# First keys on ScalarE's queue, zero products between the first scores, evenly spread weights, and the last pair but one normalized through DRAM

## The chip, the cores and the metric

The kernel runs on one core of one Trainium2 chip. The metric is the device time of one execution in microseconds (us), as the median of several. Engines are named as in the profile: PE is TensorE's matmul, PEld its weight load, DVE is VectorE, ACT is ScalarE, POOL is GpSimd, SP is SyncE. Each engine works through its own instructions strictly in the order in which the program lists them, so one that waits holds back all that stand behind it.

## What is computed

Three layers follow each other. Attention runs over 2 batches of 12 heads, 448 positions and head size 64, with a soft cap; a gated MLP with a gelu, a layer norm and a product over positions comes next; the third is a gated layer with a convolution over three positions.

```python
scores = scale * np.matmul(q, k.transpose(0, 1, 3, 2))
scores = cap * np.tanh(scores / cap)
attn = np.exp(scores - scores.max(-1, keepdims=True))
attn = attn / (attn.sum(-1, keepdims=True) + 1e-09)
x = np.matmul(attn, v)                      # heads side by side: (2, 448, 768)
h = gelu_tanh(x @ w_in); u, v = h[..., :512], h[..., 512:]
x = x + (u * (einsum('ts,bsd->btd', w_sg, layer_norm(v) * g_ln) + b_sg)) @ w_out
h = np.maximum(x @ w2_in, 0)
c = conv3(h, conv_w)                        # over positions, per channel
out = (h * sigmoid(c)) @ w2_out
```

## The kernel before

**Precision.** Every operand of the large products is split into a rounded high part and a low remainder; `mm3` and `scores` make one product of three matmuls (high by high, high by low, low by high). The weights come as 64-bit floats; `decode` turns a piece of them into such a pair in steps on ACT and DVE (`f` tiles; a piece of `w_in` is 128 rows by 512 columns).

**Attention** works on twelve pairs of heads, N = 0 to 11; pairs 0 to 5 are batch 0. `load(n)` issues five transfers on SP's queue: the queries of the two heads and three pieces of the key tile `kr`. `prep_q` and `prep_k` split them into `Q` and `K`. For pair 0 the queries are not scaled, and the high part of the keys is cast by ACT instead of DVE. A pair is done in two halves, which are the steps R = 2N and 2N+1 of the main loop. `scores(N, half)` makes the scores of two groups of keys in PSUM (`sc`, one buffer); ACT takes their tanh and then exp into `raw`. For pair 0, and for it alone, tanh and exp are done group by group (groups g = 0 to 3), and the matmuls of a group wait until the tanh of the group ahead has read the `sc` tile. `values(N, half)` multiplies `raw` with the values into `pv`, and gathers the sums of the exponentials into `su` by products with ones; for the first half DVE first adds the two groups up in `sm`. It runs one step behind `scores`, and from R = 13 on two steps behind. In the gaps PE makes the first three units of the next layer (`FILL`, tile `mo`). Ten matmuls on a tile of zeros (`wz`, written to `wps`) keep PE at work ahead of the first scores.

**Normalization.** `norm` copies `su` to `se` (DVE) and `pv` to `E` (ACT). After every second pair the sums of both go through DRAM: POOL's queue gathers them (`ss`), DVE adds the guard and takes reciprocals, POOL's queue writes them to DRAM (`d`) and broadcasts them back to 64 partitions each (`rb`, four transfers), and DVE multiplies `E` with `rb`; the product is split into `X`, the input of the next layer. These steps come 3, 4 and 11 ticks of the loop later (two ticks for each R). The last two pairs, N = 10 and 11 (`NFAST = 2`), take `norm_pe`: DVE adds the guard and takes reciprocals of the whole 128 x 224 tile, four matmuls with `sel` spread them over the partitions (`rp`, in the bank of `su`), DVE multiplies.

**Order.** The code issues work in the order of the loop; a scheduler then sets each engine's order, and `ordered` and `pin` chain some instructions to the one before. `WIN` says at which step (half steps of pairs, in pairs) each of the twelve pieces of `w_in` is requested; the decoding follows 3, 4 and 5 ticks later. `conv_w` (24 columns) and `g_ln` are requested at R = 1 by `columns`.

After attention, the units `u_unit`, `v_unit`, `sg_unit`, `o_unit`, then `h_unit` and `f_unit` are long rows of matmuls with small work on DVE and ACT beside them. The fourth `u_unit` stands right behind attention, the first `v_unit` (L585) behind the second `rp`.

Of the kernel before, what the change touches and what calls it, by code (L numbers as in the profile page):

```python
# [16 lines left out]
P = 128  # L17
# [14 lines left out]
NFAST = 2  # L32
# [7 lines left out]
WIN = (0, 1.5, 3, 4, 5, 6, 6, 8, 8.5, 9.5, 10, 10)  # L40
# [6 lines left out]
def stages(  # L47
# [169 lines left out]
    def attention(att, psa):  # L217
# [12 lines left out]
        def load(n):  # L230
            b, p = divmod(n, NPAIR)
            qr = att.tile([P, S], F32, tag="qr", name="qr", bufs=2)
            kr = kraw[n % 2]
            for h in range(2):
                r = slice(h * D, (h + 1) * D)
                nc.sync.dma_start(qr[r], qT[b, p, r, h])
            nc.sync.dma_start(kr[:D, :S], kT[b, p, :D, 0])
            nc.sync.dma_start(kr[D:, :ST], kT[b, p, D:, 1, D:])
            nc.sync.dma_start(kr[D:, S:], kT[b, p, D:, 1, :D])
            qraw[n] = qr, kr  # L240
# [23 lines left out]
        def prep_k(n):  # L264
            _, kr = qraw.pop(n)
            K = Kt[n % 2]
            lastv[0] = split(kr, K[:, 0], K[:, 1], "a" if n == 0 else "v")
# [26 lines left out]
        raws, acc, held, pairs = {}, {}, {}, []  # L294
        lastm = [None]

        def ordered(*args, **kw):

            with pin(lastm):
                lastm[0] = T.matmul(*args, **kw)  # L300


        def scores(N, half):
# [11 lines left out]
            for g in range(2 * half, 2 * half + 2):  # L315
# [11 lines left out]
                if N == 0:  # L327
                    soft(slice(t, t + (2 if g < 3 else 1)))
            if N:
                soft(slice(0, 4 - half))  # L330
# [37 lines left out]
        def norm(N, ps, su):  # L368
# [13 lines left out]
            if j == 0:  # L382
                return
            ss = att.tile([P, 14], F32, tag="ss", name="ss", bufs=2)
            G.dma_start(ss, se[::32])
            rb = att.tile([P, 2, S], F32, tag="rb", name="rb", bufs=2)

# [3 lines left out]
            def s1():  # L391
# [3 lines left out]
                ds.append(dr.tile([2, 2, 2, S // 2], F32, tag="d", name="d"))  # L395
                d = ds[0]
                G.dma_start(d.rearrange("h f j (p c) -> (h f j p) c", c=14), ss)

            def s1b():
                (d,) = ds  # L400
                for h in range(2):
                    for i in range(2):
# [5 lines left out]
            def s2():  # L408
                with pin(lastv):
                    V.tensor_tensor(out=e, in0=e, in1=rb, op=ALU.mult)  # L410
                with pin(lasta):
                    lastv[0] = split(e, X[:, 0, p - 1 : p + 1, b], X[:, 1, p - 1 : p + 1, b], "a")
# [26 lines left out]
        for R in range(2 * NN + LAGS[1]):  # L439
# [6 lines left out]
            if R < 2 * NN:  # L446
                if half == 0 and N + 2 < NN:
                    load(N + 2)
                scores(N, half)
# [430 lines left out]
```

## Time and profile before

| | |
|---|---|
| median of 3 runs | 350.95 us (349.65 to 352.41) |
| the profiled execution | 349.8 us, of which the span of the profile is 347.9 us |
| PE busy | 328.6 us, 94% of the span |
| DVE busy | 252.9 us, 73% |
| ACT busy | 225.5 us, 65% |
| POOL busy | 32.7 us, 9% |

The profile shows one execution. Times in it count from the start of the span; the 1.9 us between span and time lie outside it. A row of the timeline gives the start, the duration, the engine, the line and operation, and in brackets how long the engine had been idle before it and what ended the wait. Matmuls of one row can overlap. The granted clock of PE (PEclk) is 1.00 at 2.4 GHz and 0.50 at 1.2 GHz.

### The profile page before, as it was taken

The numbers are of one execution on the slowest core, as the hardware profiler recorded it, in microseconds if no ns is written. First come the engines' busy times: TensorE is split into PE (matmuls) and PEld (weight loads), VectorE is DVE, ScalarE is ACT, GpSimd is POOL, SyncE is SP. The second block draws the span as 40 slices with busy tenths as digits, with TensorE's granted clock in tenths as the row PEclk, the third lists the DMA queues.
The fourth block names the chain that finished last, engine by engine and source line by source line (L and its number), as shares of the span: only waits on it lengthen the run. The fifth ranks groups of instructions, "written<-read, shape, count | busy, mean of one in ns | idle before, by whom it ended". The sixth has DMA issues, their size and how long they took to land. (4 is left out here: it accounts for less than half of the span.)

```text
span 347.9 us, 5121 instructions
## 1 busy us (share of the span) xinstructions
PE 328.6 (94%) x1812; PEld 250.5 (72%) x1812; DVE 252.9 (73%) x491; ACT 225.5 (65%) x362; POOL 32.7 (9%) x67
## 2 busy tenths in 40 slices
PE   6699999997999899999999999999999999999992
PEld 4344444543446376898889999999999999999992
DVE  3365888977699545999899679997995999980000
ACT  2868899996899333766776565465775988873110
POOL 3000310403130303021110100000000000000000
PEclk9599999999999999999999999999999999999999
DMA  3895484646422213321323466000275113012211
GB/s 109 254 237 174 128 217 145 186 93 192 113 75 61 74 35 104 94 71 53 99 75 96 132 177 245 2 0 8 85 239 216 32 60 90 3 54 106 81 53 35
DMA packets 18538, 37.43 MB, mean 108 GB/s; under 512 B 3888, under 2 KB 9032, under 8 KB 18504
## 3 DMA queue, kind: packets, MB, share of 16 engines
q1 hardware_dynamic: 17192, 34.64, 32.8%
q0 software_dynamic: 1312, 2.38, 2.7%
q8 instruction: 16, 0.26, 0.3%
q14 instruction: 18, 0.15, 0.1%
HBM read 34.18 MB, written 2.79 MB: 106 GB/s over the span
## 5 line engine op out<-in xcount | busy, mean ns | idle before, releaser
L300 PE MATMUL sc<-Q,K 64*128 64x448 f32 (+1 forms) x252 | 40.5, 403 | 5.9 <-ACT raw L312 4.0
L96 PE MATMUL mo<-X,WI 128*128 128x448 f32 x126 | 46.1, 367 | 0.0
L97 PE MATMUL mo<-X,WI 128*128 128x448 f32 x126 | 45.9, 366 | 0.0
L98 PE MATMUL mo<-X,WI 128*128 128x448 f32 x126 | 45.9, 365 | 0.0
L300 PE MATMUL pv<-raw,V 128*64 128x448 f32 (+1 forms) x168 | 45.1, 579 | 0.0
L300 PEld LDWEIGHTS sc<-Q,K 64*128 64x128 f32 (+1 forms) x252 | 25.2, 193 | 20.9 <-ACT raw L312 8.1
L313 ACT ACTIVATE raw<-raw,one 128x1792 f32<-128x1792 f32 (+3 forms) x26 | 39.1, 1502 | 0.6
L138 DVE SCALAR_TENSOR_TENSOR f<-f 128x512 uint32<-128x512 uint32 (+3 forms) x57 | 30.7, 548 | 10.8 <-ACT f L131 8.2
L312 ACT ACTIVATE raw<-sc 128x1792 f32<-128x1792 f32 (+1 forms) x22 | 32.4, 1475 | 8.7 <-PE sc L300 8.7
L128 ACT ACTIVATE f<-f 128x512 f32<-128x512 f32 (+3 forms) x57 | 30.6, 542 | 10.8 <-DMA f<-in_w_out_dram 5.5
L97 PE MATMUL mo<-HG,W 128*128 128x448 f32 x96 | 34.8, 365 | 0.0
L98 PE MATMUL mo<-HG,W 128*128 128x448 f32 x96 | 34.7, 365 | 0.0
L96 PE MATMUL mo<-HG,W 128*128 128x448 f32 x96 | 34.1, 365 | 0.0
L141 DVE SCALAR_TENSOR_TENSOR f<-f 128x512 uint32<-128x512 uint32 (+3 forms) x57 | 30.7, 548 | 0.2
L300 PEld LDWEIGHTS pv<-raw,V 128*64 128x64 f32 (+1 forms) x168 | 12.0, 147 | 22.2 <-issue 18.6
L96 PEld LDWEIGHTS mo<-X,WI 128*128 128x128 f32 x126 | 23.6, 187 | 2.4 <-DVE u L177 0.4
L97 PEld LDWEIGHTS mo<-X,WI 128*128 128x128 f32 x126 | 23.7, 188 | 2.0
L98 PEld LDWEIGHTS mo<-X,WI 128*128 128x128 f32 x126 | 23.6, 188 | 2.0
L765 ACT ACTIVATE o<-mo 128x448 f32<-128x448 f32 x12 | 6.3, 540 | 26.3 <-PE mo L98 18.6
L131 ACT ACTIVATE f<-f 128x256 uint32<-128x256 uint32 (+2 forms) x44 | 22.5, 511 | 0.0
L97 PEld LDWEIGHTS mo<-HG,W 128*128 128x128 f32 x96 | 18.0, 188 | 1.4
L96 PEld LDWEIGHTS mo<-HG,W 128*128 128x128 f32 x96 | 18.0, 188 | 1.4
(140 smaller groups left out, 645.1 us busy)
## 6 DMA issues: line engine op xcount, KB each, us to landing
f<-in_w_in_dram SPq DMA_DIRECT2D x24, 512.0 KB, 4.8
f<-in_w_out_dram SPq DMA_DIRECT2D x24, 256.0 KB, 4.6
V<-in_vL_dram SPq DMA_DIRECT2D x12, 256.0 KB, 3.9
f<-in_w_out_dram SPq DMA_DIRECT2D x8, 384.0 KB, 3.1
qr<-in_qT_dram SPq DMA_DIRECT2D x24, 112.0 KB, 3.5
out_dram<-o SPq DMA_DIRECT2D x12, 224.0 KB, 1.9
rb<-d POOLq DMA_DIRECT2D x20, 112.0 KB, 3.8
kr<-in_kT_dram SPq DMA_DIRECT2D x12, 112.0 KB, 3.1
```

The lines of the kernel that those rows point to most:

```text
L96: matmul(ps, lhsT=whi, rhs=xhi, start=start, stop=False)
L97: matmul(ps, lhsT=whi, rhs=xlo, start=False, stop=False)
L98: matmul(ps, lhsT=wlo, rhs=xhi, start=False, stop=stop)
L128: A.activation(f(h), f(h), AF.Copy, scale=2.0**-112)
L131: A.activation(l, l, AF.Copy, scale=0.93 * 2.0**-29)
L138: V.scalar_tensor_tensor(out=l, in0=h, scalar=3, in1=l, op0=ALU.logical_shift_left, op1=ALU.bitwise_or)
L141: V.scalar_tensor_tensor(out=l, in0=h, scalar=0x80000000, in1=l, op0=ALU.bitwise_and, op1=ALU.bitwise_or)
L300: lastm[0] = T.matmul(*args, **kw)
L312: A.activation(raw[:, t], ps[:, t, :S], AF.Tanh, **sc)
L313: lasta[0] = A.activation(raw[:, t], raw[:, t], AF.Exp, scale=capc)
L765: A.activation(o, ps, AF.Copy, scale=0.5)
```

## The change

The three key transfers of pair 0 are issued by ACT's queue instead of SP's, and the high part of these keys is cast by DVE like all others. After each of the first two groups of scores PE gets five matmuls on the tile of zeros (`idle`). The first half of the values of pair 0 moves from behind its last group of scores to between groups 2 and 3. `WIN` asks for a piece of `w_in` every 0.9 pairs. `NFAST` becomes 1: pair 10 is normalized through DRAM, by itself, with half-size `ss`, `d` and two `rb` transfers.

```diff
-NFAST = 2
+NFAST = 1
+IDLE = 5
-WIN = (0, 1.5, 3, 4, 5, 6, 6, 8, 8.5, 9.5, 10, 10)
+WIN = tuple(0.9 * j for j in range(12))
...
-            nc.sync.dma_start(kr[:D, :S], kT[b, p, :D, 0])
-            nc.sync.dma_start(kr[D:, :ST], kT[b, p, D:, 1, D:])
-            nc.sync.dma_start(kr[D:, S:], kT[b, p, D:, 1, :D])
+            dma = (nc.sync if n else nc.scalar).dma_start
+            dma(kr[:D, :S], kT[b, p, :D, 0])
+            dma(kr[D:, :ST], kT[b, p, D:, 1, D:])
+            dma(kr[D:, S:], kT[b, p, D:, 1, :D])
...
-            lastv[0] = split(kr, K[:, 0], K[:, 1], "a" if n == 0 else "v")
+            lastv[0] = split(kr, K[:, 0], K[:, 1])
...
+        idle = psm.tile([P, 512], F32, tag="mo", name="idle")[:, :S]
...
-        def scores(N, half):
+        def scores(N, half, between=None):
...
                 if N == 0:
                     soft(slice(t, t + (2 if g < 3 else 1)))
+                    for _ in range(IDLE if g < 2 else 0):
+                        ordered(idle, lhsT=wz[:, :P], rhs=wz, start=True, stop=True)
+                if between and g == 2:
+                    between()
...
-            if j == 0:
+            last = N == B * NPAIR - NFAST - 1
+            if j == 0 and not last:
                 return
-            ss = att.tile([P, 14], F32, tag="ss", name="ss", bufs=2)
-            G.dma_start(ss, se[::32])
+            m = j + 1
+            ss = att.tile([P, 14], F32, tag="ss", name="ss", bufs=2)[:, : 7 * m]
+            G.dma_start(ss, se[::32, :m])
             rb = att.tile([P, 2, S], F32, tag="rb", name="rb", bufs=2)
+            eb, rb = e[:, :m], rb[:, :m]
...
-                    for i in range(2):
+                    for i in range(m):
...
-                scores(N, half)
+                if R == 1:
+                    scores(N, half, lambda: values(0, 0))
+                    done += 1
+                else:
+                    scores(N, half)
```

The order on PE at the start, from the products of zeros to the second pair's first scores (`K_87` holds the keys of pair 0, `K_88` those of pair 1; `x` counts instructions in a row), before:

```order
L279 MATMUL wps<-wz 128x448 x10
L300 MATMUL sc<-Q,K_87 128x448 x21
L300 MATMUL pv<-raw,V 64x448 x4
L300 MATMUL su<-sm,ones_138 32x224 x4
L300 MATMUL sc<-Q,K_88 128x448 x12
```

and now:

```order
L283 MATMUL wps<-wz 128x448 x10
L305 MATMUL sc<-Q,K_87 128x448 x6
L305 MATMUL idle<-wz 128x448 x5
L305 MATMUL sc<-Q,K_87 128x448 x6
L305 MATMUL idle<-wz 128x448 x5
L305 MATMUL sc<-Q,K_87 128x448 x6
L305 MATMUL pv<-raw,V 64x448 x4
L305 MATMUL su<-sm,ones_138 32x224 x4
L305 MATMUL sc<-Q,K_87 128x448 x3
L305 MATMUL sc<-Q,K_88 128x448 x12
```

The one row of 21 score matmuls is cut into four groups, with zero products behind the first two and the first values and sums ahead of the last.

The order on DVE at the start, from the constants (`one`) to the first `sm`; `f_155` (`f_156` in the changed kernel) is the first piece of `w_in` and the 24 columns of `f_189` (`f_200`) are `conv_w`, before:

```order
L205 TENSOR_TENSOR one<-one 128x1
L207 TENSOR_SCALAR one<-one 128x1
L93 TENSOR_TENSOR K_87<-kr_89,K_87 128x512
L258 TENSOR_SCALAR Q<-qr,one 128x448
L259 SCALAR_TENSOR_TENSOR Q<-qr,one,Q 128x448
L90 CAST K_88<-kr_90 128x512
L93 TENSOR_TENSOR K_88<-kr_90,K_88 128x512
L133 TENSOR_SCALAR f_155<-f_155 128x512
L133 TENSOR_SCALAR f_189<-f_189 128x24
L333 TENSOR_TENSOR sm<-raw 128x896
```

and now:

```order
L260 TENSOR_TENSOR Q<-qr,Q 128x448
L209 TENSOR_SCALAR one<-one 128x1
L92 CAST K_87<-kr_89 128x512
L95 TENSOR_TENSOR K_87<-kr_89,K_87 128x512
L262 TENSOR_SCALAR Q<-qr,one 128x448
L263 SCALAR_TENSOR_TENSOR Q<-qr,one,Q 128x448
L92 CAST K_88<-kr_90 128x512
L95 TENSOR_TENSOR K_88<-kr_90,K_88 128x512
L135 TENSOR_SCALAR f_156<-f_156 128x512
L135 TENSOR_SCALAR f_200<-f_200 128x24
L342 TENSOR_TENSOR sm<-raw 128x896
```

The cast of the first keys has come to DVE, behind the constants and the queries; `sm` stands behind the same work on `conv_w` as before.

The order on DVE in the middle, at the multiplication of pairs 2 and 3 (`E<-E,rb`) and what stands between it and the next `sm`, before:

```order
L410 TENSOR_TENSOR E<-E,rb 128x896
L138 SCALAR_TENSOR_TENSOR f_626<-f_626 128x512
L141 SCALAR_TENSOR_TENSOR f_624<-f_624 128x512
L141 SCALAR_TENSOR_TENSOR f_626<-f_626 128x512
L147 CAST WI_76<-f_624 128x512
L147 CAST WI_77<-f_626 128x512
L150 TENSOR_TENSOR WI_76<-f_624,WI_76 128x512
L333 TENSOR_TENSOR sm<-raw 128x896
```

and now:

```order
L423 TENSOR_TENSOR E<-E,rb 128x896
L149 CAST WI_77<-f_618 128x512
L152 TENSOR_TENSOR WI_77<-f_618,WI_77 128x512
L342 TENSOR_TENSOR sm<-raw 128x896
L92 CAST K_88<-kr_90 128x512
```

Of two pieces of `w_in` that were decoded there together, one is left; the other has moved behind the next `sm`.

The order on PE at the end of attention, around the normalization of pair 10, before:

```order
L300 MATMUL su<-raw,ones_136 32x224 x2
L300 MATMUL su<-raw,ones_137 32x224 x2
L300 MATMUL pv<-raw,V 64x448 x4
L429 MATMUL rp<-r,sel 64x224 x4
L300 MATMUL su<-sm,ones_138 32x224 x4
L300 MATMUL mo<-X,WI_76 128x448 x18
```

and now:

```order
L305 MATMUL su<-raw,ones_136 32x224 x2
L305 MATMUL su<-raw,ones_137 32x224 x2
L305 MATMUL pv<-raw,V 64x448 x4
L305 MATMUL su<-sm,ones_138 32x224 x4
L305 MATMUL mo<-X,WI_76 128x448 x18
```

The four `rp` matmuls of pair 10 are gone, and the sums of pair 11 stand right behind its values.

## Rows read from the trace of the kernel before

**Rows 1.** Busy time by stretch: PE, PEld, DVE, ACT, POOL, granted clock, DMA share.

```profile
20.00:40.00 20.00, 20.00 (x154) 9.06 (x154) 12.22 (x29) 16.49 (x15) 1.31 (x2) 1.00 0.60 172
...
60.00:80.00 20.00, 17.82 (x126) 8.69 (x124) 16.70 (x32) 18.99 (x17) 3.70 (x6) 1.00 0.56 147
80.00:100.00 20.00, 18.31 (x138) 8.93 (x138) 15.19 (x31) 15.43 (x15) 3.80 (x7) 1.00 0.44 130
...
160.00:347.90 187.90, 181.61 (x885) 165.77 (x883) 136.92 (x272) 110.91 (x234) 4.58 (x9) 1.00 0.28 89
```

**Rows 2.** The same view of the first scores.

```profile
1.38:5.48 4.10, 4.10 (x10) 3.14 (x10) 0.40 (x2) 0.64 (x1) 2.46 (x15) 1.00 0.42 118
...
7.33:8.53 1.20, 1.14 (x6) 0.48 (x6) 1.16 (x3) 0.00 (x0) 0.00 (x0) 1.00 0.37 102
8.53:9.63 1.10, 0.00 (x0) 0.00 (x0) 1.07 (x3) 1.02 (x2) 0.00 (x0) 0.63 0.96 335
9.63:11.12 1.49, 1.49 (x6) 0.84 (x6) 0.53 (x1) 1.02 (x1) 0.00 (x0) 0.50 0.98 377
...
16.23:19.27 3.04, 3.04 (x9) 0.78 (x9) 2.71 (x6) 1.99 (x4) 0.00 (x0) 0.53 0.85 221
```

**Rows 3.** Timeline of the start, all engines.

```profile
1.39 0.73 POOL L269 DMA_DIRECT2D one<-in_cap_dram  x1
...
3.28 0.60 SPq L239 DMA_DIRECT2D kr<-in_kT_dram  x1
...
6.50 0.20 ACT L206 ACTIVATE one<-one 128x1 f32<-128x1 f32 x1 [4.49 <-DVE one L205]
...
7.33 1.20 PE L300 MATMUL sc<-Q,K 64*128 64x448 f32 x6 [1.85 <-ACT K L92]
...
11.99 0.43 SPq L123 DMA_DIRECT2D f<-in_conv_w_dram  x1
...
16.34 0.63 ACT L312 ACTIVATE raw<-sc,one 128x448 f32<-128x448 f32 x1 [0.51 <-PE sc L300]
16.57 0.18 DVE L133 TENSOR_SCALAR f<-f 128x24 uint32<-128x24 uint32 x1 [4.76 <-DMA f<-in_conv_w_dram]
16.65 1.08 DVE L333 TENSOR_TENSOR sm<-raw 128x896 f32<-128x896 f32 x1
...
19.79 1.48 PE L300 MATMUL sc<-Q,K 64*128 64x448 f32 x12
```

**Rows 4.** Transfers issued in the first 20 us: kilobytes, median us to landing.

```profile
f<-in_conv_w_dram SPq DMA_DIRECT2D x1, 24.0 KB, 4.6
one<-in_cap_dram POOLq DMA_DIRECT2D x1, 0.5 KB, 3.4
```

**Rows 5.** Timeline of the middle, PE and DVE.

```profile
72.03 1.09 DVE L410 TENSOR_TENSOR E<-E,rb 128x896 f32<-128x896 f32 x1 [2.59 <-DMA rb<-d]
...
73.65 1.31 DVE L141 SCALAR_TENSOR_TENSOR f<-f 128x512 uint32<-128x512 uint32 x2
...
76.76 1.72 PE L300 MATMUL pv<-raw,V 128*64 128x448 f32 x8
...
80.95 0.59 PE L300 MATMUL su<-sm,ones 128*32 128x224 f32 x8 [2.47 <-DVE se L380]
```

**Rows 6.** Timeline of the end of attention.

```profile
110.11 3.82 PE L300 MATMUL mo<-X,WI 128*128 128x448 f32 x18
...
118.15 2.41 POOL L403 DMA_DIRECT2D rb<-d  x4 [1.46 <-DMA d<-ss]
...
119.33 0.98 PE L429 MATMUL rp<-r,sel 128*64 128x224 f32 x8 [1.00 <-DVE r L423]
...
121.02 0.59 PE L300 MATMUL su<-sm,ones 128*32 128x224 f32 x8 [0.72 <-DVE E L433]
...
133.04 0.62 DVE L433 TENSOR_TENSOR E<-E,rp 128x448 f32<-128x448 f32 x1 [1.17 <-PE rp L429]
```

**Rows 7.** The tile `rb`: us from issue to landing of its transfers.

```profile
DMA to landing us min/median/max: 2.8/3.8/5.8
```

More of the change, by code (lines that the diff above doesn't have):

```diff
@@ L394, in s1 @@
                 V.reciprocal(out=ss, in_=ss)
-                ds.append(dr.tile([2, 2, 2, S // 2], F32, tag="d", name="d"))
+                ds.append(dr.tile([2, 2, m, S // 2], F32, tag=f"d{m}", name="d"))
                 d = ds[0]
-                G.dma_start(d.rearrange("h f j (p c) -> (h f j p) c", c=14), ss)
+                G.dma_start(d.rearrange("h f j (p c) -> (h f j p) c", c=7 * m), ss)
             def s1b():
@@ L409, in s2 @@
                 with pin(lastv):
-                    V.tensor_tensor(out=e, in0=e, in1=rb, op=ALU.mult)
+                    V.tensor_tensor(out=eb, in0=eb, in1=rb, op=ALU.mult)
                 with pin(lasta):
-                    lastv[0] = split(e, X[:, 0, p - 1 : p + 1, b], X[:, 1, p - 1 : p + 1, b], "a")
+                    lastv[0] = split(eb, X[:, 0, p - j : p + 1, b], X[:, 1, p - j : p + 1, b], "a")
             later(3, s1)
```

## The prediction

> **What bounds the kernel now.** I read the busy time by stretch first. PE is at work in all of 20 to 40 us and in nearly all of the long last stretch, loses 2.18 of 20 us at 60 to 80 and 1.69 at 80 to 100 [rows 1]. So a change pays where PE waits ahead of its full stretches, and what it takes out of such a wait moves everything behind it. The same view of the first scores shows the granted clock: 1.00 while the first group of scores runs, 0.63 in the wait behind it, then 0.50, and 0.53 over the first values and sums [rows 2]; the fall is at about 8.8 us (a mix of 1.00 and 0.50 over 1.10 us that gives 0.63). The timeline of the start then tells what the first pair waits for; those of the middle and of the end name PE's longest waits in attention, for DVE's copy of the sums and around the first `rp`. The profiled execution took 349.8 us, 1.15 below the median of 350.95; the sum is made against 349.8.
>
> **First keys.** The first score started at 7.33, released by ACT's cast, and that cast stood behind ACT's exp of the guard at 6.50, which waited for DVE's constants [rows 3]. The keys had landed earlier: their last issue was at 3.28, 0.60 us each [rows 3]. Moved to ACT, the three issues come some 1.3 us sooner; ACT's table load goes behind them and is hidden, since nothing else is asked of ACT before the exp. What is left is DVE's row: the cap lands at 1.39 + 3.4 = 4.8 [rows 3, 4], then the constants, the two query steps, the guard and the new cast follow each other. The first steps of this row took no more than the 1.7 us from the landing to the exp, the whole no more than the 2.5 to the first score [rows 3]; I take 2.05, so the first score comes at 6.85 and its group is over at 7.95 instead of 8.53. The ends are a gain of 0.7 and none.
>
> **Zero products and clock.** At the full clock eighteen matmuls of this size take 3.82 us [rows 6], so five take 1.06, and the wait that they stand in is 1.10 [rows 2]: they cost nothing there. At half clock ten took 4.10 [rows 2], so five take 2.05 and each block would push the next group by 0.95. Their operands are zeros, but so are those of the ten ahead of the scores, and the clock stood at 1.00 after those. A group of six takes 1.49 at half clock [rows 2] and about 0.75 at full (twelve take 1.48 [rows 3]). With the clock kept, ACT becomes the row that counts: from 8.0 us on tanh and exp, some 1.03 each (ACT is busy for 1.02 of the 1.10 in which it does one [rows 2]), follow each other without a gap, so the second exp ends at 12.15; the third group is over at 11.9. The four values products start at 12.2 and, with 1.72 us for this step [rows 5], end at 13.9.
>
> **The sums that follow them.** Here is the point on which the start turns. The sums need `sm`, and on DVE `sm` still stands behind the first step on `conv_w`. That step waited 4.76 us for its transfer and ran at 16.57, `sm` right after it at 16.65 [rows 3]; before, PE came to the sums so late that this cost nothing. Now it is late next: the sums stand ahead of the fourth group on PE. The transfer was issued at 11.99 and took 4.6 [rows 3, 4]. SP has three issues of 0.60 less ahead of it, of which I give back 0.3 for waits on earlier transfers: issue at 10.4, landing at 15.0. Then `sm` 15.1 to 16.2 (1.08 [rows 3]), sums to 16.8 (0.59 [rows 5]), the three matmuls of group 3 to 17.6, tanh of 0.63 [rows 3] to 18.3, and the second pair's scores start there instead of at 19.79. Gain of the whole start: **1.5**. The ends: 3.9 if `conv_w` is not in the way (sums to 14.5, scores at 15.9), nothing if it lands as late as now. I take the middle because the transfer's queue is ahead by what I can count, while the DMA engines are the busier for it: their share is already 0.96 and 0.98 in the two stretches from 8.53 [rows 2]. The first keys' 0.5 is inside this, not beside it.
>
> **The clock in the new hole.** PE is idle from 13.9 to 16.2, works 1.4 and waits 0.7 for the tanh. In the middle a hole of 2.47 us [rows 5] left the clock at 1.00 [rows 1]; at the start 1.85 us of waiting, 1.20 of work and another wait were followed by a fall [rows 2, 3]. The rows thus point both ways, and I take no fall, at a price of 0, with an upper end of 2.8: group 3 0.7 longer, and some 4.1 us at half pace (as long as the ten products of zeros ran before the clock stood at 1.00 [rows 2]), 2.1. The Trainium skill ("TensorE: Matmul & The Clock Gate", section "Why this matters for your kernels") says that the engine keeps its clock unless an idle gap between bursts is longer than any in this start. By that rule the sum below stays, and by the rows of the start it would be up to 2.8 higher. But by the rule there would have been no fall before either, and the trace shows one, so for short bursts between waits the measurement decides against it.
>
> **Pair 10 through DRAM.** Out go the wait for its reciprocals (1.00), `rp` (0.98) and the wait of pair 11's sums for the bank (0.72) [rows 6]: **2.7**. Its bank is now freed by DVE's short copy, made while PE is still at pair 11's values. If that copy were late, the 0.72 would stay: 2.0. What is added is hidden: one copy on DVE, two small steps, four POOL issues, and a chain with a due time. POOL finishes the broadcasts of pairs 8 and 9 at 120.56 [rows 6]; then `d` (its landing took about 2 us there: the broadcasts began 1.46 after its issue ended [rows 6]), two broadcasts issued at 122.6 and 123.2, landing 3.8 later, 5.8 at most [rows 7]: 127.0, at most 129.0. DVE's multiplication for pair 11, which frees the bank for the first `v_unit`, was at 133.04 [rows 6] and comes at 130.3. Even the slowest broadcast leaves time for pair 10's 0.62 us. The step costs nothing unless `ss` and `d` land late too.
>
> **Even spread.** No decoding goes away; twelve pieces stay. What counts is what stands on DVE between the multiplication that waits for `rb` (72.03) and the copy for which PE waits until 80.95 [rows 5]. Three shifts and masks of 0.65 each [rows 5] leave that place, and a cast and a subtraction that I estimate at 0.4 each: 2.75. Two first steps and a query step come in, by the same sizes 1.45. So the copy comes 1.3 earlier; a weight step that now stands ahead of a tanh on ACT gives some 0.4 back. Further on, DVE gets a double set of decoding steps (four shifts and masks in a row) between two `sm`; it fits where DVE has waited for `rb`. Net **0.9**. Ends: 3.9, if all of PE's idle time in 60 to 100 went [rows 1], and a loss of 0.5 if the second `rb` still lands where it did and the later decoding runs into it.
>
> **Sum.** 1.5 + 2.7 + 0.9 = 5.1, so 349.8 - 5.1 = 344.7. The runs of before lie up to 2.6 above the profiled execution, their median 1.15, and I let a part of that stay: 0.3, **345.0**.
>
> **Rivals.**
> *The clock falls in the new hole.* Of the 2.8 above I take 2.4, since the wait for the tanh hides a part: 347.4. For it: the fall at 8.8 came with as much work around it. Against: the hole of 2.47 us in the middle.
> *The zero products do not hold the clock*, so that the change does not do what it says. Two blocks 0.95 longer, groups and values at half pace as now: scores of pair 1 at about 20.3, 0.5 later than before; 349.8 + 0.5 - 2.7 - 0.9 = 346.7, with the 0.3 it is 347.0. Against: the ten zero products brought the clock up.
> *`conv_w` is not in the way*, because its transfer was held up by what SP issued rather than by the engines. Scores at 15.9 and 2.4 more gained: 345.0 - 2.4 = 342.6.
> *Late broadcasts, the slower side.* DVE stands in a row behind each multiplication with `rb`; if the evenly spread pieces load the DMA engines just when `rb` is under way and each of the four middle broadcasts takes 5.8 instead of 3.8 [rows 7], DVE loses 2 us four times, the copies of the sums come as much later, and PE waits for them: 8 us, 353. It decides from 1.5 us each, where the 5.95 between 345.0 and the median are gone. Against: the pieces before were loaded in pairs, which is worse for the same engines.
>
> **How the numbers follow.** Chances: forecast 0.45, clock in the hole 0.22, zero products 0.11, `conv_w` out of the way 0.12, late broadcasts 0.05, and 0.05 for a middle that loses 1 to 3 us (about 348). A measurement here can tell about 1% from no change, so faster means below 347.4. All of the forecast and of `conv_w`, half of the clock's fall and two thirds of the zero products lie there: 0.45 + 0.12 + 0.11 + 0.07, rounded to 0.76. Slower by over 1% is the broadcasts' 0.05; same is 0.19. The range 342.2 to 348.2 takes in the early `conv_w` and both clock cases with their ends.
>
> **What will show it.** The first score at 6.8 to 7.0 and zero products of 0.21 us each; PEclk 1.00 from 8.5 to 13 us; DVE's step on `conv_w` near 15.0, with `sm` and PE's sums right behind it; the second pair's scores at 18.3; PE's wait for the copy in the middle near 1.2 us instead of 2.47; no `rp` for pair 10 and no wait of DVE for its `rb`; the first `v_unit` some 5 us earlier than before. Wrong would make it: a clock of 0.50 anywhere behind 13 us, a new wait of PE on `se` or `sm` of over 2 us, or DVE waiting for pair 10's broadcasts.

## The result and the profile after

The changed kernel takes 346.28 us, the median of 4 runs (346.03 to 347.37), against 350.3 for the kernel before on the same chip: ratio 0.987, interval 0.983 to 0.991. Run again among the experiments it took 347.02 (6 runs, 345.39 to 349.73) against 352.1: 0.989, 0.984 to 0.993. The profiled execution took 346.11 with a span of 344.2, 3.7 less than before. Ratios here and below leave out executions over 1.5% above the fastest of their kernel, of which there are two: one of a_nfast2 (354.15) and the profiled one of e_warm15 (351.67).

Three marks on PE cut each trace into pieces that can be compared: **P**, the start of pair 1's scores; **M**, from there to the first values of pair 11; **E**, from there to the end of the span. Before they are 19.79 [rows 3], 96.81 (pair 11's first values begin at 116.60) and 231.3; after, 17.65, 97.69 and 228.86: the start gains 2.14, the middle loses 0.88, the end gains 2.44. The kernel before was profiled once, so how far its own start and middle differ between executions is not known.

**The start.** Timeline of the changed kernel, PE and DVE, for [rows 3]:

```profile
5.66 0.39 DVE L259 CAST Q<-qr 128x448 fp32r<-128x448 f32 x1 [0.22 <-DMA qr<-in_qT_dram]
...
7.22 1.20 PE L305 MATMUL sc<-Q,K 64*128 64x448 f32 x6 [1.77 <-DVE K L92]
...
8.35 1.94 PE L305 MATMUL idle<-wz 128*128 128x448 f32 x5
...
10.22 1.49 PE L305 MATMUL sc<-Q,K 64*128 64x448 f32 x6
...
13.88 1.72 PE L305 MATMUL pv<-raw,V 128*64 128x448 f32 x8
...
14.13 0.18 DVE L135 TENSOR_SCALAR f<-f 128x24 uint32<-128x24 uint32 x1 [3.59 <-DMA f<-in_conv_w_dram]
14.22 1.08 DVE L342 TENSOR_TENSOR sm<-raw 128x896 f32<-128x896 f32 x1
...
15.54 0.59 PE L305 MATMUL su<-sm,ones 128*32 128x224 f32 x8
...
17.65 1.49 PE L305 MATMUL sc<-Q,K 64*128 64x448 f32 x12 [0.72 <-ACT raw L317]
```

The first score is only 0.11 earlier than before. The first block of five zero products takes 1.94 us, most of it at half pace (granted clock 0.58 below), instead of the 1.06 of the forecast; the group behind it takes 1.49. PE idles no longer between the groups, but it works mostly at half clock there. The same in the busy time by stretch (columns as in rows 1), for [rows 2]:

```profile
7.22:8.42 1.20, 1.15 (x7) 0.55 (x7) 1.17 (x3) 0.00 (x0) 0.00 (x0) 1.00 1.04 407
8.42:10.22 1.80, 1.80 (x6) 1.17 (x5) 1.70 (x4) 1.72 (x2) 0.00 (x0) 0.58 0.96 316
10.22:11.72 1.50, 1.50 (x8) 0.91 (x7) 0.32 (x1) 0.33 (x1) 0.00 (x0) 0.50 0.50 165
11.72:13.07 1.35, 1.35 (x5) 0.98 (x5) 0.00 (x0) 1.28 (x2) 0.00 (x0) 0.85 0.66 132
60.00:80.00 20.00, 17.49 (x118) 8.34 (x120) 15.38 (x30) 17.09 (x16) 4.41 (x7) 0.92 0.62 157
80.00:100.00 20.00, 19.61 (x143) 9.75 (x136) 17.28 (x33) 16.07 (x15) 3.69 (x6) 0.99 0.38 93
```

The clock falls at about 8.7 us as before, but it is back at about 12, so that the first values take 1.72 us, where before they still ran at half pace [rows 2]. The step on `conv_w` comes at 14.13 and `sm` at once after it; the sums do not wait. The last two stretches answer to [rows 1]: 60 to 80 us has lost another 0.33 us of PE and some of its clock, 80 to 100 has won 1.30.

**The middle.** Timeline, DVE, ACT and PE, for [rows 5]:

```profile
56.78 1.08 DVE L95 TENSOR_TENSOR X<-E,X 128x896 fp32r<-128x896 f32 x1
...
57.78 0.23 DVE L406 TENSOR_SCALAR ss<-ss,one 128x14 f32<-128x14 f32 x1
...
71.47 1.09 DVE L423 TENSOR_TENSOR E<-E,rb 128x896 f32<-128x896 f32 x1 [3.90 <-DMA rb<-d]
...
72.60 0.95 ACT L94 ACTIVATE X<-E 128x896 fp32r<-128x896 f32 x1 [2.46 <-DVE E L423]
...
73.45 0.66 ACT L130 ACTIVATE f<-f 128x512 f32<-128x512 f32 x1
...
74.02 1.27 ACT L317 ACTIVATE raw<-sc 128x1344 f32<-128x1344 f32 x1
...
75.33 1.50 PE L305 MATMUL sc<-Q,K 64*128 64x448 f32 x12 [2.19 <-ACT raw L317]
...
76.76 3.09 PE L305 MATMUL pv<-raw,V 128*64 128x448 f32 x8
...
79.78 0.86 PE L305 MATMUL su<-sm,ones 128*32 128x224 f32 x8
```

DVE waits 3.90 us for the broadcasts (before 2.59), and behind the multiplication with `rb` ACT has its copy into `X` and a weight step ahead of pair 7's tanh. PE waits 2.19 us for that tanh; its clock falls (granted 0.50 over 78 to 80 us), and the values that took 1.72 before take 3.09. The wait for the copy `se` (2.47 before) is gone. Pair 8's scores begin at 75.33, before at 75.34: all that the start had gained is gone here.

**The end of attention.** Timeline, PE and DVE, for [rows 6]:

```profile
115.34 1.72 PE L305 MATMUL pv<-raw,V 128*64 128x448 f32 x8
...
116.99 0.58 PE L305 MATMUL su<-sm,ones 128*32 128x224 f32 x8
...
127.76 0.61 DVE L423 TENSOR_TENSOR E<-E,rb 128x448 f32<-128x448 f32 x1
...
129.79 0.47 PE L603 MATMUL mo<-WI,X 128*128 128x512 f32 x1 [0.84 <-DVE E L446]
```

and the two of before that answer to its first and its last:

```profile
116.60 1.72 PE L300 MATMUL pv<-raw,V 128*64 128x448 f32 x8
...
133.81 0.47 PE L585 MATMUL mo<-WI,X 128*128 128x512 f32 x1 [0.82 <-DVE E L433]
```

From the first values of pair 11 to the first `v_unit` (now L603) it takes 14.45 us, before 17.21. Pair 11's sums follow the values without a wait, the broadcast for pair 10 has landed when DVE gets to it (no bracket at 127.76).

### The profile page after: what moved, and what is told of

Its sections match the earlier page's. It is cut to its first block, busy times and chain, and to the rows that moved or that the text cites. A ratio compares the mean times of both kernels' runs of the same rounds, so it can differ in the third digit from the quotient of the medians.

```text
span 344.2 us, 5129 instructions
## 1 busy us (share of the span) xinstructions
PE 329.7 (96%) x1814; PEld 251.5 (73%) x1814; DVE 252.6 (73%) x493; ACT 224.9 (65%) x361; POOL 35.2 (10%) x71
## 3 DMA queue, kind: packets, MB, share of 16 engines
q0 software_dynamic: 1472, 2.61, 3.2%
## 4 chain that ended last, share of the span: by engine, by line
PE 76%; issue 11%; DMA 5%; DVE 3%; POOL 2%; SPq 1%; ACT 0%; DVEq 0%; POOLq 0%; ACTq 0%
PE mo L98 17%; PE mo L99 17%; PE mo L100 17%; PE pv L305 5%; PE sc L305 4%; PE mo L603 3%; PE mo L605 3%; PE mo L604 3%; PE mo L305 3%; PE su L305 2%; DMA d<-ss 2%; DMA rb<-d 2%; POOL rb L416 2%; DMA ss<-se 1%; PE idle L305 1%
## 5 line engine op out<-in xcount | busy, mean ns | idle before, releaser
L305 PE MATMUL sc<-Q,K 64*128 64x448 f32 (+1 forms) x252 | 39.3, 395 | 5.3 <-ACT raw L317 3.5
L305 PEld LDWEIGHTS sc<-Q,K 64*128 64x128 f32 (+1 forms) x252 | 24.5, 188 | 20.2 <-issue 6.7
```

## The experiments

Twelve runs were made in three groups of four, each group on one chip beside the kernel before (351.32, 352.1 and 352.25 there); kernels of different groups are compared by their ratio to it. The groups are a_nfast2 to d_late, r_after to k_all, and the last four. "Zero block" is the time of the first five zero products, "rb" what DVE waited for broadcasts in all. Times are medians of all runs, the columns behind the ratios are of one profiled execution each.

| kernel | time, us | ratio (interval) | zero block | P | M | E | rb |
|---|---|---|---|---|---|---|---|
| before | 350.3 | | | 19.79 | 96.81 | 231.3 | 5.4 |
| changed | 346.28 | .987 (.983 to .991) | 1.94 | 17.65 | 97.69 | 228.86 | 7.2 |
| a_nfast2 | 349.53 | .994 (.990 to .998) | 2.17 | 19.22 | 97.90 | 231.78 | 7.3 |
| b_oldwin | 348.23 | .993 (.989 to .996) | 2.23 | 19.66 | 98.21 | 228.73 | 4.8 |
| c_noidle | 347.64 | .991 (.988 to .994) | none | 18.70 | 96.33 | 228.97 | 5.6 |
| d_late | 342.07 | .974 (.969 to .978) | 2.23 | 18.97 | 93.15 | 228.58 | 0 |
| r_after | 347.02 | .989 (.984 to .993) | 2.23 | 18.79 | 96.05 | 228.66 | 5.3 |
| e_warm15 | 347.52 | .985 (.981 to .990) | 1.31 | 19.42 | 101.63 | 228.75 | 9.0 |
| f_conv | 346.43 | .985 (.981 to .989) | 2.23 | 17.50 | 97.95 | 229.05 | 7.2 |
| k_all | 340.07 | .968 (.964 to .972) | 1.27 | 16.14 | 93.10 | 228.56 | 0 |
| s_swap | 343.37 | .977 (.973 to .980) | 1.29 | 18.05 | 93.43 | 228.92 | 0 |
| k_keysp | 341.05 | .969 (.965 to .973) | 1.28 | 16.33 | 95.39 | 228.58 | 0 |
| k_noidle | 341.99 | .969 (.966 to .973) | none | 17.54 | 93.99 | 228.67 | 0 |
| k_all_oldwin | 340.67 | .967 (.964 to .970) | 1.28 | 15.81 | 94.22 | 228.97 | 1.4 |

**a_nfast2: pair 10 by `rp` again.**

```
-NFAST = 1
+NFAST = 2
```

> One part undone: the last pair but one has its reciprocals again by the matrix product on TensorE, as before the change (NFAST 2). My theory: the DRAM way of pair 10 is worth 2.7 us by itself, because TensorE then doesn't wait for that pair's sum at the end of the head loop; all up to pair 9 stays as in the changed kernel. So the score of pair 8 begins at 75.3 us as there, the last pair's sum is multiplied at 121.0 - 1.3 = 119.7 us, the first step of the next stage comes 2.8 us later than the changed kernel's 129.8, and the time is 346.3 + 2.7 = 349.0 us. Rival: the DRAM way only moved the wait, to the reciprocals of the last pair, and what it saves is below 1 us; then 346.3 to 347.3 us.

349.53 us. E is 2.92 longer than in the changed kernel, and from pair 11's first values to the first `v_unit` the trace takes 17.22 us, against 14.45 or 14.46 in every kernel with the DRAM way. So that part is worth 2.77, and the rival falls. The start brought a surprise; DVE's step on `conv_w`, and PE's sums:

```profile
15.78 0.18 DVE L135 TENSOR_SCALAR f<-f 128x24 uint32<-128x24 uint32 x1 [5.23 <-DMA f<-in_conv_w_dram]
...
17.11 0.59 PE L305 MATMUL su<-sm,ones 128*32 128x224 f32 x8 [1.65 <-DVE sm L342]
```

Here `conv_w` landed 1.65 us later than in the changed kernel's profile, though issued at 10.67 against 10.50, and the sums waited 1.65 for `sm`.

**b_oldwin: the weight pieces at the times of before.**

```
-WIN = tuple(0.9 * j for j in range(12))
+WIN = (0, 1.5, 3, 4, 5, 6, 6, 8, 8.5, 9.5, 10, 10)
```

> One part undone: the pieces of the output's weight are prepared at the uneven times of before; first keys, zero products, the values between the score groups and pair 10 stay. My theory: in the changed kernel a piece at its new time stands on VectorE and ScalarE ahead of pair 7's tanh, behind a multiplication that waits 3.9 us for its broadcasts, so TensorE waits 2.19 us for ScalarE at 75.3 us, and its clock falls to .50 behind that; the even spread costs 0.9 us up to pair 11. With the old times that wait is below 0.5 us, the values of pair 7 take 1.7 us instead of 3.1, but the wait of before at pair 7's sum (2.47 us, by VectorE) comes back in part: pair 8's scores at 73.2 us, and the time 346.3 - 0.9 = 345.4 us (344.5 to 346.0). Rival: the even spread is a gain of 0.9 as predicted, and the late scores at 75.3 come of the broadcasts, wherever the pieces stand: then 346.5 to 347.5 us, with the wait at pair 8's scores still about 2 us.

348.23 us, and M did not get shorter: 98.21. The wait for `se` came back whole (2.48), behind DVE's wait of 3.27 for `rb`, and this time the clock fell behind it. My theory of the moment, that the new times make the wait, fell: with either spread PE waits for the broadcasts; only the queue in which that shows differs. That the even spread gains 0.9 is not shown either: M with old times is 96.81 and 98.21, with new ones 97.69, 96.05, 97.90, 96.33 and 97.95 in the five kernels that are alike there.

**c_noidle: no zero products.**

```
-IDLE = 5
+IDLE = 0
```

> One part undone: no zero products between the first score groups; the rest as in the changed kernel. There the clock fell to .50 within the first block of them, 8.4 us into the trace, and the two blocks took 1.94 and 1.50 us. Theory one: the products don't hold the clock but give it back sooner (at 12 us, before the change at 19.1): without them the groups wait for nothing but ScalarE and VectorE, the clock stays at .50 until about 18 or 19 us, the first values and the first sum run at half clock (3.4 instead of 1.7 us), and pair 1's scores begin at 18.6 to 19.8 us instead of 17.65; the time is 347.3 to 348.4 us, less whatever a later wait gives back. Theory two: the blocks only stand in the way of the score groups behind them, which begin 1 to 2 us earlier without them; the tanh chain on ScalarE sets pair 1's scores and these begin at 17.0 to 17.7; then 345.6 to 346.3 us.

347.64 us, not to be told from the changed kernel (.989 in r_after). P is 18.70, while six executions with zero products and the same start (the changed kernel twice, a_nfast2, b_oldwin, d_late, s_swap) have 17.65 to 19.66, 18.72 on the mean. PE:

```profile
9.51 1.49 PE L305 MATMUL sc<-Q,K 64*128 64x448 f32 x6 [1.10 <-ACT raw L317]
...
13.52 2.69 PE L305 MATMUL pv<-raw,V 128*64 128x448 f32 x8
```

The first values start 2.7 us before their old place (16.23 [rows 2]) because they now stand ahead of group 3, and that without a zero product. Both theories miss a part: the groups come sooner, as the second says, and the clock comes back later (the values take 2.69), as the first says. Together nothing is left. Against the kernel before, whose second group began at 9.63 [rows 2], P is 1.09 sooner here with groups only 0.12 sooner, so most of this comes with the move of the values.

**d_late: the multiplication with `rb` two ticks later.**

```
-            later(11, s2)
+            later(13, s2)
...
-        for _ in range(9):
+        for _ in range(11):
```

> One size changed: the multiplication of a pair's values by the broadcast reciprocals is put two steps of the head loop later (13 instead of 11, and two more empty steps at the loop's end). In the changed kernel it waits 3.9 us for pair 2 and 3's broadcasts on VectorE at 71.5 us, and 2.55 us for pair 4 and 5's at 89.7 us, with ScalarE's copy and pair 7's tanh behind it. My theory: what blocks the middle is this wait in front of the tanh; 3 us later the broadcasts have landed, the wait is below 0.5 us, pair 8's scores begin at 73.2 to 73.7 instead of 75.3 us with the clock at 1.00 behind them; at the end of the head loop pair 10's multiplication isn't what the next stage waits for longer than 1 us. Time 344.3 to 345.5 us. Rival: VectorE is behind by its own work at that place, not by the wait, so that the same lateness shows as a wait for VectorE somewhere between 72 and 82 us: 346.0 to 346.6 us, or above if the two steps at the end are paid in full (up to 349).

342.07 us, better than the theory said: M is 93.15 and DVE never waits for `rb`. But the multiplication of pairs 2 and 3 was not later for it. DVE:

```profile
52.32 0.23 DVE L406 TENSOR_SCALAR ss<-ss,one 128x14 f32<-128x14 f32 x1 [0.88 <-DMA ss<-se]
...
68.82 1.09 DVE L423 TENSOR_TENSOR E<-E,rb 128x896 f32<-128x896 f32 x1
```

In the changed kernel the guard was added to the sums of pairs 2 and 3 (L406) at 57.78 and the multiplication came at 71.47; here at 52.32 and 68.82. The reason is an order: a block of two pairs follows the last by 8 ticks of the loop, so its first step on `ss`, 3 ticks on, falls on the same tick as the multiplication of the block before, 11 on. What was entered first is issued first, and the chain on DVE then puts the guard behind that multiplication and behind the subtraction into `X` (56.78 above), which itself needs ACT's copy (ended at 55.88). With 13 the guard goes ahead. s_swap separates the two. The kernel before has the order of the changed one; DVE there:

```profile
58.91 1.08 DVE L93 TENSOR_TENSOR X<-E,X 128x896 fp32r<-128x896 f32 x1
59.91 0.22 DVE L393 TENSOR_SCALAR ss<-ss,one 128x14 f32<-128x14 f32 x1
```

**r_after: the changed kernel again**, the measure for the next three on their chip.

> The changed kernel once more, as the kernel that the others are held against on one chip, and to see how much its start and its middle differ between executions. In the five kernels with this start so far pair 1's scores began at 17.65, 19.22, 19.66, 18.70 and 18.97 us, with the step on the convolution's weight at 14.1 to 16.2 us. If the start is a matter of when that weight lands, pair 1's scores begin in this execution anywhere from 17.6 to 19.7 us, and 1.5 us or more behind the convolution's step if that comes after 15 us. Time 346.3 to 348.5 us.

347.02 us; P 18.79, M 96.05. PE at the start:

```profile
7.11 1.49 PE L305 MATMUL sc<-Q,K 64*128 64x448 f32 x6 [1.63 <-DVE K L92]
8.53 2.23 PE L305 MATMUL idle<-wz 128*128 128x448 f32 x5
```

Already the first group takes 1.49 us, which is half pace; in the first profile it took 1.20. So here the clock did not fall in the zero block, it had not yet come up: the trace's record of the clock begins with a rise at 13.38 us, and no matmul ahead of 13 us ran at full pace. The same holds for a_nfast2 and b_oldwin (first group 1.49, first record a rise at 10.77 and 13.46). In the first profile, d_late and f_conv the clock did rise, at 5.30, 4.22 and 4.57, and fell at 8.71, 7.64 and 7.98.

Pair 8's scores begin at 75.40. The broadcasts were issued 1.24 us later than in the first profile (63.98 against 62.74), the multiplication came at the same time:

```profile
63.98 2.53 POOL L416 DMA_DIRECT2D rb<-d  x4 [1.96 <-DMA d<-ss]
...
71.48 1.09 DVE L423 TENSOR_TENSOR E<-E,rb 128x896 f32<-128x896 f32 x1 [2.68 <-DMA rb<-d]
```

In the kernel before, the changed one twice, a_nfast2, b_oldwin, c_noidle and f_conv P lies anywhere from 17.50 to 19.79, but these scores start at 74.95 to 76.16, at 75.33 and 75.34 with P at 17.65 and 19.79 (the long execution of e_warm15, at 79.55, is left out). Their broadcasts were issued at 62.74 to 65.47, and the multiplication came at 71.09 to 72.62. The middle hangs on the broadcasts, as d_late and s_swap show, and most of what the start gains ahead of them is lost there. Why the landing varies less than the issue is not settled; the DMA share of the changed kernel is 1.09 and 1.05 at 66 to 70 us, which would fit crowded engines, but no run shows that this is the cause.

**e_warm15: five more products ahead of the first scores.**

```
-WARM = 10
+WARM = 15
```

> 15 instead of 10 warming products ahead of the first scores; the rest as in the changed kernel. Theory one: the clock falls in the first zero block because TensorE stood still for 1.8 to 2.2 us ahead of the first scores. Five more products of .21 us fill 1.1 us of that, the clock stays at 1.00, the first zero block takes 1.1 us instead of 1.9 to 2.2 and the first values come at 12.2 to 12.8 instead of 13.5 to 15.2 us. The step on the convolution's weight (14.1 to 16.2 us) then holds the sum in each execution, so that pair 1's scores begin 3.4 us behind it, at 17.6 to 19.6 us, and the time gains 0 to 0.8 us against the changed kernel on this chip. Theory two: the hole isn't what lowers the clock; the blocks take 1.9 us and more as before, and nothing changes.

347.52 us. The profile is of an execution of 351.67, the longest of its six (the others 344.85 to 348.27), so only the start is read, and it may not be that of the others. PE:

```profile
12.66 1.72 PE L305 MATMUL pv<-raw,V 128*64 128x448 f32 x8
16.43 0.85 PE L305 MATMUL su<-sm,ones 128*32 128x224 f32 x8 [2.05 <-DVE sm L342]
17.21 1.49 PE L305 MATMUL sc<-Q,K 128*128 128x448 f32 x3
19.42 2.61 PE L305 MATMUL sc<-Q,K 64*128 64x448 f32 x12 [0.72 <-ACT raw L317]
```

What theory one says of the start came about: the blocks run at full pace (the first takes 1.31) and the first values come at 12.66. That the hole alone was to blame is not shown, since five more products do two things: they shorten the hole (0.49 ahead of the first score), and they give the clock time to come up (its rise is recorded at 6.38, while they still ran). Then `conv_w` holds `sm`, the sums wait 2.05, and the clock falls behind this hole: the sums, group 3 and pair 1's scores take 0.85, 1.49 and 2.61 us instead of 0.59, 0.88 and 1.49. P is 19.42 in this execution, no gain. By the ratio, 0.985 against 0.989 of r_after and inside the intervals, no gain is shown either.

**f_conv: `conv_w` out of the way.**

```
-            if R == 1:
+            if R == 3:
                 columns(att)
```

> The gains and the convolution's weight are asked for and decoded two half pairs later (with pair 1's second half), so that no step on them stands on VectorE ahead of the first sum; the rest as in the changed kernel. Theory one (the prediction's): the sum is held by this step in most executions. Without it the sum follows the second exponential, the first sum's product has no wait, and pair 1's scores begin at 17.6 to 18.0 us in every execution, where zero blocks at half clock are what is left; the gain is 0.5 to 1.5 us against the changed kernel on this chip unless the middle eats it. Theory two: the chain of TensorE at half clock sets the start and the sum is never late by more than a few tenths; then pair 1's scores begin where they do now, and the time is the same.

346.43 us. P is 17.50 with no wait for `sm`, with a first zero block still at half pace. The 0.985 against 0.989 of r_after is inside the intervals; M gave the start's gain back (97.95, with the clock fallen behind a wait of 2.00 for pair 7's tanh).

**k_all: the three edits of e_warm15, f_conv and d_late together.**

> Three edits together: 15 warming products, the convolution's weight two half pairs later, the multiplication by the broadcast reciprocals two steps later. If the theories on the start (a hole lowers the clock, and the convolution's step holds the sum) are both right, neither edit alone shows what both do: pair 1's scores begin at 15.8 to 16.4 us. From there to the values of pair 11 the later multiplication alone took 93.15 us, against 97.7 in the changed kernel, so these come at 109.3 instead of 115.3 us and the time is 342.1 - 2.8 = 339.3 us (338.3 to 340.5). Rival: the middle hangs on transfers that don't come sooner when the start does, so that the 2.8 us are lost there again: 342 us.

340.07 us, faster than both kernels: 0.968 (0.964 to 0.972) of the one before, and 0.980 of the changed one on this chip (340.07 / 347.02). PE:

```profile
7.21 1.20 PE L305 MATMUL sc<-Q,K 64*128 64x448 f32 x6 [0.23 <-DVE K L92]
8.34 1.27 PE L305 MATMUL idle<-wz 128*128 128x448 f32 x5
...
12.37 1.72 PE L305 MATMUL pv<-raw,V 128*64 128x448 f32 x8
14.02 0.59 PE L305 MATMUL su<-sm,ones 128*32 128x224 f32 x8
...
16.14 1.48 PE L305 MATMUL sc<-Q,K 64*128 64x448 f32 x12 [0.73 <-ACT raw L317]
```

The blocks run at full pace (1.27), the first values at 12.37, the sums right behind them, and P is 16.14. M stays at 93.10, so with the wait for the broadcasts gone the start's gain reaches the end. The rival falls. P of 16.14 is near the 15.9 that the prediction gave for a `conv_w` out of the way with the clock kept.

**s_swap: only the order.**

```
-            later(3, s1)
+            due.setdefault(now[0] + 3, []).insert(0, s1)
```

> The changed kernel with one order swapped and no step moved in time: where the steps on a new pair's sums (add the guard, reciprocal, store to DRAM) fall on the same step of the head loop as the last pairs' multiplication by their broadcasts, they now come first. In the changed kernel they stand behind that multiplication and behind VectorE's subtraction, which waits for ScalarE's copy: the sums of pairs 2 and 3 landed at about 52 us, and the guard was added at 57.8. In the kernel with the later multiplication this came along: 52.3 us. Theory one: this order is the whole cause of the late broadcasts, each block's reciprocals waiting for the block before; the swap alone brings the broadcasts 4 to 5 us sooner, the multiplication at 67 to 69 us has no wait, pair 8's scores begin 1 to 2 us sooner (73.0 to 74.3 us), and the time is 342.0 to 344.0 us, ratio .973 to .978, near the kernel with the later multiplication (.9735). Theory two: the later multiplication is what gained; the swap brings the broadcasts sooner but VectorE now waits about 1 us for the sums, ahead of the same multiplication, and the time stays at 345.5 to 347 us, ratio above .982.

343.37 us: theory one. No step is moved in time, M is 93.43, against 93.15 with the later multiplication. DVE, and PE's pair 8:

```profile
51.32 0.23 DVE L406 TENSOR_SCALAR ss<-ss,one 128x14 f32<-128x14 f32 x1 [0.80 <-DMA ss<-se]
...
67.67 0.23 DVE L406 TENSOR_SCALAR ss<-ss,one 128x14 f32<-128x14 f32 x1 [0.91 <-DMA ss<-se]
...
67.87 1.09 DVE L423 TENSOR_TENSOR E<-E,rb 128x896 f32<-128x896 f32 x1
...
73.48 1.50 PE L305 MATMUL sc<-Q,K 64*128 64x448 f32 x12
```

The guard's step waits 0.80 and 0.91 us for its sums on DVE; M shows no cost of it. The multiplication follows at once, where the changed kernel waited 3.90. The clock kept full pace at the start here (first group 1.20, zero block 1.29), though start and hole (1.64 ahead of the first score) are those of r_after (1.63): here its rise is recorded at 6.03, inside the hole, there not before 13.38.

**k_keysp: k_all with the first keys by SP, cast by ACT.**

```
-            dma = (nc.sync if n else nc.scalar).dma_start
+            dma = nc.sync.dma_start
...
-            lastv[0] = split(kr, K[:, 0], K[:, 1])
+            lastv[0] = split(kr, K[:, 0], K[:, 1], "a" if n == 0 else "v")
```

> The kernel with the three edits (15 warming products, convolution's weight later, multiplication later), with the first keys asked for by SyncE's queue again and cast by ScalarE, as before the change. Theory one: the queue of the first keys is worth nothing, because the cast waits for the data, and queries and keys come through the same DMA engines: the first scores begin at 7.1 to 7.5 us (7.21 with ScalarE's queue), pair 1's at 16.0 to 16.5, and the time is 340.1 us, within 0.5, ratio .966 to .970. Theory two, by the step of the prediction: keys by ScalarE's queue land 0.5 us sooner, so without it first scores begin at 7.6 to 7.8 us and pair 1's at 16.5 to 16.8, the time 340.6 us.

341.05 us, first score at 7.38 instead of 7.21, P 16.33 instead of 16.14. This is within theory one, but single executions do not bound it at 0.2: with the keys on ACT's queue and the same 15 products, the first score came at 7.46 in e_warm15, 7.21 in k_all, 7.11 in k_noidle and 6.88 in k_all_oldwin. In time (0.969 against 0.968 and 0.967) no gain shows. DVE and ACT:

```profile
5.13 0.39 DVE L259 CAST Q<-qr 128x448 fp32r<-128x448 f32 x1 [3.81 <-DMA qr<-in_qT_dram]
...
6.70 0.63 ACT L94 ACTIVATE K<-kr 128x512 fp32r<-128x512 f32 x1
```

With the keys on SP the queries are cast at 5.13, with both queues at work at 5.65 in k_all (5.31 to 5.89 in the four). So what the keys gain the queries lose at least in part, and the keys' cast starts at 6.70 here, 6.75 there. The Trainium skill ("DMA: Bandwidth & Descriptors", section "Issuing engines are not separate DMA queues") says that transfers of all issuing engines share the same 16 engines, so that a second issuer saves only the issuing; the trace agrees.

**k_noidle: k_all without zero products.**

```
-IDLE = 5
+IDLE = 0
```

> The kernel with the three edits without the zero products between the first score groups. There the clock stayed at 1.00 through the start with them. Theory one: with the hole ahead of the first scores filled, the groups of .88 us with waits of about 1.1 us for ScalarE between them keep the clock as well as the zero products do: pair 1's scores begin at 16.1 to 16.5 us, the time is 340.1 us within 0.6. Theory two: the waits between the groups lower the clock, so a group takes 1.49 and the first values 3.1 us, pair 1's scores begin at 17.5 to 19 us, and the time is 341.5 to 343 us.

341.99 us; by the ratios (0.969, 0.968) not to be told from k_all, but the trace shows theory two. PE:

```profile
9.41 0.88 PE L305 MATMUL sc<-Q,K 64*128 64x448 f32 x6 [1.10 <-ACT raw L317]
11.39 1.49 PE L305 MATMUL sc<-Q,K 64*128 64x448 f32 x6 [1.10 <-ACT raw L317]
12.81 2.69 PE L305 MATMUL pv<-raw,V 128*64 128x448 f32 x8
```

The waits of 1.10 lower the clock by the third group (1.49, values 2.69), P is 17.54, 1.40 later than with them. So with 15 products ahead of the first scores, zero products between the groups kept the clock (no block of the four kernels that have both ran at half pace), and in the one execution without them it fell.

**k_all_oldwin: k_all with the old times of the weight pieces** (the edit of b_oldwin).

> The kernel with the three edits, with the pieces of the output's weight at the uneven times of before. Theory one: what differed in the middle between the two spreads was only which engine's queue stood behind the wait for the broadcasts; with that wait gone the spread is worth nothing, the middle from pair 1's scores to pair 11's values takes 93.1 us as with the even spread, and the time is 340.1 us within 0.5, ratio .966 to .970. Theory two, by the prediction: two pieces at once keep VectorE or ScalarE late at one place, 0.9 us, which shows as a wait of TensorE in the middle: 341 us, ratio above .970.

340.67 us, ratio 0.967 against 0.968: theory one. M is 94.22, inside the 93.10 to 95.39 of the kernels with even times and no wait for `rb`; one of its own multiplications waits 1.4.

## Why the prediction was right, and where it was wrong

Forecast 345.0, measured 346.28, within the range. By the marks the change gave 3.70 us of span in the first profile (2.14 - 0.88 + 2.44) and 4.40 in r_after (1.00 + 0.76 + 2.64), against a sum of 5.1. Only the term for pair 10 came true in size and mechanism; that the rest came out near is partly luck. Of the prediction's own signs, PEclk of 1.00 from 8.5 to 13 us failed (0.50 to 0.85 after 8.42), and a clock of 0.50 behind 13 us, which it named as a sign of being wrong, appeared in the middle.

- **Start, 1.5.** Measured 2.14 and 1.00: right in size, by another road. *First keys*: 0.5 forecast; the first score came at 7.08 to 7.45 in the eight executions with this start, 7.22 on the mean, against 7.33 before: some 0.1 is left of it, less than the executions differ. That step took DVE's row from the cap's landing (4.8 forecast, 5.03 measured) without asking whether the queries come later when keys come beside them: their cast moved from 5.08 to 5.66. *Zero products*: cost 0 forecast, on the premise that the clock stands at 1.00 when the ten products ahead of the scores have run. It did not hold in seven executions with this start and zero products: in three the clock had not come up (r_after, a_nfast2, b_oldwin), in three it came up and fell (the first profile, d_late, f_conv), with first blocks of 1.94 to 2.23 us; in s_swap alone it stood. (The row from which the prediction took half pace, ten products in 4.10 us [rows 2], shows it by their duration; the granted clock printed there is 1.00.) The condition of the rival "they do not hold the clock" was met there, but its price was not right: the values' move ahead of group 3, which the prediction counted inside the start, still gained (c_noidle). *`conv_w`*: landing forecast at 15.0; its step ran at 14.1 to 16.2 in the traces. It holds the sums in some executions (1.65 in a_nfast2, 1.90 in s_swap) and in others, as in the first profile, not, because half clock has delayed PE as much. Removing one of the two limits alone (e_warm15, f_conv) gains no time that can be measured.
- **Clock in the new hole, 0.** True of the changed kernel, but not for the reason given: the hole of 2.3 us that was forecast ahead of the sums was not there (no wait in the first profile, 0.23 in r_after), because PE came later. Where it was there, the rows go both ways: in s_swap, behind 1.90, the clock stood; in the profiled execution of e_warm15, behind 2.05, it fell and cost 0.26 + 0.61 + 1.12 = 2.0 us. The rule of the Trainium skill ("TensorE: Matmul & The Clock Gate", section "Why this matters for your kernels") that the prediction weighed would have had no fall in any of these starts. The falls recorded at 7.64 to 8.82 us in five of them (before, the first profile, c_noidle, d_late, f_conv), behind waits of 1.77 to 2.24, decide against it here.
- **Pair 10, 2.7.** 2.76 in both profiles (17.21 - 14.45), 2.77 by undoing it. The rest of E is 0.32 and 0.12 longer, a stretch that the change doesn't touch.
- **Even spread, 0.9.** This step of the prediction failed: M was 0.88 longer and 0.76 shorter in two executions of the changed kernel, and the spread is worth nothing that could be shown, with the wait for `rb` (b_oldwin) or without it (k_all_oldwin). The reckoning counted DVE steps between the multiplication and the copy `se`. But the wait ahead of the multiplication sets the place, and it grew from 2.59 to 3.90 when PE came earlier (2.68 in r_after). The sentence "it fits where DVE has waited for `rb`" also left out ACT: the weight step behind the same wait stands ahead of a tanh, at a cost given as 0.4, and PE waited 2.19 and lost its clock for a while (1.14 and no loss in r_after).
- **What was not seen**: the broadcasts come late because each block's reciprocals are issued behind the block before's multiplication. The order was the same before the change (d_late above), but the swap was tried in the changed kernel alone. Taking this away is worth 2.6 to 4.5 us of M (96.05 and 97.69 against 93.43 and 93.15), more than the start and the spread together.

## What to carry to other kernels

Follow a gain forward to the next wait that isn't released by the engine that gained; if a transfer ends that wait, the gain stops there. Where two periodic chains fall on the same step of a loop, look which is issued first: a chain that starts behind the end of the one before it makes every wait longer. And read a start with a wavering clock from several executions: P of one start spread over 2 us, more than the terms that were being weighed.

## What the hardware did unexpectedly

- With ten zero products ahead of the first scores, the clock had come up by the first score in six of nine profiled executions and not in three (r_after, a_nfast2, b_oldwin), with the same work on PE. With fifteen it had in all five, its rise recorded at 4.55 to 6.97 us.
- The length of a hole alone does not tell whether the clock falls behind it: in the middle it fell behind 2.48 us in b_oldwin and behind 2.19 in the first profile, and not behind 2.47 before the change [rows 5].
- In r_after the granted clock reads 1.00 over 8.3 to 13 us, while the five zero products take 2.23 us, which is half pace. The clock record of that trace begins at 13.38, and the view prints 1.00 where there is no record. The durations of known matmuls are the surer sign.
- Matmuls on zeros raised and kept the clock here: in eleven executions it rose before any other matmul had run, and with fifteen ahead of the first score and the blocks between groups it stayed at full pace through the groups in all four kernels that had both.
